# One load queue in order of need, and one chunk transposed by DMA, in a fused spectral filter and gated feed-forward kernel on Trainium2

## The chip, the cores and the metric

The kernel runs on one core of a Trainium2 chip. A core has five engines that run their own instruction streams and meet at semaphores: TensorE (PE, matmuls; PEld is its weight load), VectorE (DVE), ScalarE (ACT), GpSimd (POOL) and SyncE (SP, which here only issues DMAs). The metric is the device time in microseconds (us); the median of several runs is given. The profile describes one execution.

## The reference, cut to what matters

The input x has 2048 rows of 512 values, bfloat16. It is normalised by rows, and the result goes through two branches that are added to x: a filter in the two-dimensional Fourier domain, and a gated feed-forward layer with 1792 hidden values.

```python
xn = layernorm(x)                                  # rows of 512
A  = irfft2(rfft2(xn) * (w_r + 1j * w_i))          # 2048 x 257 spectrum
h  = gelu(xn @ w_gate) * (xn @ w_up)               # 2048 x 1792
B  = h @ w_down                                    # 2048 x 512
out = x + A + B
```

## The kernel before

The 2048 rows lie in SBUF as 16 tiles of 128 rows (x_sb, index j); four tiles make a chunk (index m, or b in the feed-forward part). Each tile is loaded in two halves of 64 partitions (load_x, with b = 0 and 1), because the halves come from different parts of the rows in HBM.

For each tile the row statistics are taken on DVE (ln_stat, L380; ln_aggr, L384 and L387), the reciprocal root on POOL (L388), and the normalised tile is written by DVE to xn (ln_norm, L392), a buffer of four tiles that lives in the tile cmx. Both branches want xn transposed, with the 512 values on partitions: the tile xnT. The first two tiles are transposed one by one (trans1, L1005, copied out of PSUM at L1012 and L1014), the others by trans (L402): PE transposes through an identity matrix into PSUM, then DVE (L412) or ACT (L414) copies to xnT. In this kernel xnT is laid out as [partition, 4 blocks of the 512 values, 2048 rows], so that the 512 rows of one chunk lie in a row for each of the four blocks.

From xnT the two branches go on. The feed-forward part takes, for each chunk b and each of 14 hidden blocks fc, a gate (four matmuls over the blocks of 512, L868, followed by gelu on ACT, L871) and an up (four matmuls, L883, multiplied with gelu's output on DVE, L889, into hT). The first six blocks of chunk 0 are done in two halves: first for the two first tiles, while tiles 2 and 3 are still being loaded and transposed. The products with w_down are made from sums and differences of blocks of hT and w_down (product, L772; sum_01, L705; sums_T, L734). The spectral part starts with butter (DVE, L422, L423, L425, L426), which adds and subtracts halves of xnT into the tile fold; unit_D (L439 to L443) is a matmul with a table fd, once a tile; units_A goes on with the table am (L471 to L474), and writes to the scratch scr1 in HBM, which load_tv reads back into tv. Later units B, C, E and F finish the branch, and unit_B's output is multiplied with the spectral weights W, loaded by load_W into a ring of four slots (32 loads on POOL's queue and 32 on SP's). keep_256 copies one column of a slot aside on POOL.

The order of the instructions on every engine is the order in which the program calls op. Semaphore waits are made from the keys that each op reads and writes. The main loop calls gate and up in turn, and after each of them a counter called the hook is raised; the list plan says which other calls are put in at which hook (at(h, call)). So a hook is a place in the order, about one gate or up apart. In chunk 0 the hooks 0 to 27 are passed, in chunk 1 those from 28. For the last chunk, m = 3, the norms are at hooks 28 and 29, the two transposes at 33 and 34, the butterflies at 35 and 36, and unit_D from 39.

The loads at the start are issued on two queues: SP takes one half of tiles 0 and 1, up weights for fc 0 to 2, one half of tiles 2 and 3, and up weights for fc 3 to 5; ACT takes the other halves and the gate weights in the same manner. SP then goes on with tiles 4 to 7, the table fd, weights 6 to 9, tiles 8 to 11, am, weights 10 to 13 and tiles 12 to 15. Before the first transposes PE does twelve matmuls on a tile of zeros (warm, L375).

Of the kernel before, what the change touches and what calls it, by code (L numbers as in the profile page):

```python
# [214 lines left out]
def bass_parallel_sum__spectral_gfnet__glu_gated_geglu__prompt_kernel(  # L215
# [27 lines left out]
    with ExitStack() as es:  # L243
# [4 lines left out]
        op = pr.op  # L248

        x_sb = sb("x_sb", [P, NJ, D], BF16)  # L250
        xnT = sb("xnT", [P, 4, S], F16)
        arena = sb("arena", [P, 8192], F16)
        am = arena[:, 0:3072].rearrange("p (j c) -> p j c", j=NJ)
        fold = [arena[:, 4096 + 2048 * i:6144 + 2048 * i].rearrange("p (a c) -> p a c", a=4) for i in range(2)]
# [94 lines left out]
        op("dve", lambda e: e.memset(dumm[:], 0.0), w=["dumm"])  # L349
        op("pool", lambda e: e.memset(mhalf[:], -0.5), w=["mhalf"])  # L350
        op("pool", lambda e: e.dma_start(ident[:], c_id.ap()), w=["ident"], dma=True)
        for b, eng, t, v, nm in ((0, "sp", wu_sb, wuv, "wu"), (1, "act", wg_sb, wgv, "wg")):
            load_x(0, 2, b, eng)
            load_w(t, v, nm, 0, 3, eng)
            load_x(2, 2, b, eng)
            load_w(t, v, nm, 3, 6, eng)
        op("act", lambda e: e.activation(warm_o[:], mhalf[:, 0:1], ACT.Gelu_apprx_tanh), r=["mhalf"], w=["warm_o"])
        load_x(4, 4, 0, "sp")
        load_x(4, 4, 1, "sp")
# [35 lines left out]
        def trans(m, dcs, jjs, eng="dve"):  # L395
            bk = take(1, 0.45, 1.2)
            def f(e):
                ins = None
                for a, dc in enumerate(dcs):
                    for c, jj in enumerate(jjs):  # L400
                        i = a * len(jjs) + c
                        ins = e.transpose(bank_h(bk)[:, i * P:(i + 1) * P], xn[:, jj, dc * P:(dc + 1) * P], ident[:])  # L402
                return ins
            op("pe", f, r=["ident"] + [("xn", jj) for jj in jjs], w=[("ps", bk)])
            w = len(jjs) * P
            c0 = m * 512 + jjs[0] * P
            n = len(dcs)
            dst = xnT[:, dcs[0]:dcs[0] + n, c0:c0 + w]
            src = bank_h(bk)[:, 0:n * w].rearrange("p (a c) -> p a c", a=n)
            ks = [("xnT", m, dc, jj) for dc in dcs for jj in jjs]  # L410
            if eng == "dve":
                op("dve", lambda e: e.tensor_copy(dst, src), r=[("ps", bk)], w=ks)  # L412
            else:
                op("act", lambda e: e.activation(dst, src, ACT.Copy), r=[("ps", bk)], w=ks)  # L414

        def butter(m, part):
            f = fold[m % 2]
            k = ("fold", m % 2)
            sl = slice(m * 512, (m + 1) * 512)
            xk = [("xnT", m, dc, jj) for dc in range(4) for jj in range(4)]  # L420
            if part == 0:
                op("dve", lambda e: e.tensor_tensor(ev1, xnT[:, 0:2, sl], xnT[:, 2:4, sl], ALU.add), r=xk, w=["ev1"])  # L422
                op("dve", lambda e: e.tensor_tensor(f[:, 2:4, :], xnT[:, 0:2, sl], xnT[:, 2:4, sl], ALU.subtract), r=xk, w=[k + (2,), k + (3,)])  # L423
            else:
                op("dve", lambda e: e.tensor_tensor(f[:, 0, :], ev1[:, 0, :], ev1[:, 1, :], ALU.add), r=["ev1"], w=[k + (0,)])  # L425
                op("dve", lambda e: e.tensor_tensor(f[:, 1, :], ev1[:, 0, :], ev1[:, 1, :], ALU.subtract), r=["ev1"], w=[k + (1,)])  # L426
# [225 lines left out]
               r=r + keys + [("x", j, 0), ("x", j, 1)], w=keys)  # L652

        eb7 = [early[:, 1792 * k:1792 * k + 1792].rearrange("p (f c) -> p f c", f=7) for k in range(4)]
        xb = xnT[:].rearrange("p d s -> p (d s)")
        cb = cmx[:]

        def ssum(b, k, f0, f1):
            if b == 2:
                return eb7[k][:, f0:f1, :]  # L660
            if k == 3:
                v = cb[:, 256 * f0:256 * f1]
            elif f1 <= 6:
                v = xb[:, 2048 * k + 256 * f0:2048 * k + 256 * f1]
            else:
                v = xb[:, 2048 * 3 + 256 * k:2048 * 3 + 256 * k + 256]
            return v.rearrange("p (f c) -> p f c", c=256)

        def s_keys(b, k, f0, f1):
# [45 lines left out]
        def s01(b, p, k, f0, f1):  # L715
            q = b == 0 and p == 1
            if k == 0 and b + p == 0:
                v = twh[:, 1024 + P * f0:1024 + P * f1]
            elif k == 0:
                v = arena[:, 7168 + P * f0:7168 + P * f1]  # L720
            else:
                assert f1 <= 4 or f0 >= 4
                o = P * (f0 % 4)
                if q and k in (1, 3):
                    v = fd[:, o:o + P * (f1 - f0)] if f0 >= 4 else dumm[:, o:o + P * (f1 - f0)]
                else:
                    row = 2 * (k == 2) + (f0 >= 4)
                    v = xb[:, 2048 * row + o:2048 * row + o + P * (f1 - f0)]
            return v.rearrange("p (f c) -> p f c", c=P)

        def sums_T(k):
# [127 lines left out]
        def gate(b, fc, jjs=(0, 1, 2, 3)):  # L859
            k = gun[0]  # L860
            n = len(jjs) * P
            c0 = b * 512 + jjs[0] * P
            bg = take(1, 0.0017 * n)

            def fn(e):
                ins = None
                for dc in range(4):
                    ins = e.matmul(bank(bg)[:, 0:n], wg_sb[:, dc, fc * P:(fc + 1) * P], xnT[:, dc, c0:c0 + n], start=(dc == 0), stop=(dc == 3))  # L868
                return ins
            op("pe", fn, r=[("wg", fc)] + [("xnT", b, dc, jj) for dc in range(4) for jj in jjs], w=[("ps", bg)])  # L870
            op("act", lambda e: e.activation(gl[k % 3][:, 0:n], bank(bg)[:, 0:n], ACT.Gelu_apprx_tanh), r=[("ps", bg)], w=[("gl", k % 3)])  # L871

        def up(b, fc, jjs=(0, 1, 2, 3), wait=False):
            k = gun[0]
            gun[0] += 1
            n = len(jjs) * P
            c0 = b * 512 + jjs[0] * P
            bu = take(1, 0.0017 * n, 2.2)

            def fn(e):  # L880
                ins = None
                for dc in range(4):
                    ins = e.matmul(bank(bu)[:, 0:n], wu_sb[:, dc, fc * P:(fc + 1) * P], xnT[:, dc, c0:c0 + n], start=(dc == 0), stop=(dc == 3))  # L883
# [55 lines left out]
            at(10 + 2 * i, (load_late, wd_sb[:, f0:f1, :], wdv[:, f0:f1, :], [("wd", fc) for fc in range(f0, f1)]))  # L939
        at(18, (load_late, be[:], c_be.ap(), ["be"]))  # L940
        at(19, (load_late, mm[:], c_mm.ap(), ["mm"]))
        for s, h0 in enumerate((20, 27, 34, 53, 61, 66, 70, 75)):
            for i, t in enumerate(load_W(s)):
                at(h0 + i // 2, t)
            at(89 + s // 2 if s > 3 else (47, 48, 49, 58)[s], (keep_256, s))
        cmv = c_cm.ap().rearrange("p (h r c) -> p h r c", h=NJ, r=2)
        for i, h0 in enumerate((54, 57, 63, 68)):
            hs = slice(4 * i, 4 * i + 4)
# [2 lines left out]
        for m in range(1, 4):  # L951
            a = (5, 15, 23)[m - 1]
            t = (16, 25, 33)[m - 1]
            for i in range(4):
                at(a + i, (ln_stat, 4 * m + i))
            at(a + 3, (ln_aggr, 4 * m, 4))
            for i in range(4):
                at(a + 5 + i // 2, (ln_norm, 4 * m + i))
            at(t, (trans, m, (0, 1), (0, 1, 2, 3)))
            at(t + 1, (trans, m, (2, 3), (0, 1, 2, 3), "act"))  # L960
            at(t + 2, (butter, m, 0))
            at(t + 3, (butter, m, 1))
        at(3, (butter, 0, 0))
# [35 lines left out]
        def trans1(j, engs):  # L999
            for i, eng in enumerate(engs):  # L1000
                bk = take(1, 0.12, 1.0)
                def f(e, i=i, bk=bk):
                    ins = None
                    for a in range(2):
                        ins = e.transpose(bank_h(bk)[:, a * P:(a + 1) * P], xn[:, j, (2 * i + a) * P:(2 * i + a + 1) * P], ident[:])  # L1005
                    return ins
                op("pe", f, r=["ident", ("xn", j)], w=[("ps", bk)])
                dst = xnT[:, 2 * i:2 * i + 2, j * P:(j + 1) * P]
                src = bank_h(bk)[:, 0:256].rearrange("p (a c) -> p a c", a=2)
                ks = [("xnT", 0, 2 * i + a, j) for a in range(2)]  # L1010
                if eng == "dve":
                    op("dve", lambda e, dst=dst, src=src: e.tensor_copy(dst, src), r=[("ps", bk)], w=ks)  # L1012
                else:
                    op("act", lambda e, dst=dst, src=src: e.activation(dst, src, ACT.Copy), r=[("ps", bk)], w=ks)  # L1014
# [108 lines left out]
```

## Time and profile before

| What | Value |
|---|---|
| median of 5 runs | 183.21 us (182.83 to 184.56) |
| profiled execution, own time | 183.1 us |
| its span (first to last instruction of the core) | 181.3 us |
| granted TensorE clock | 0.998 |
| PE, DVE, ACT, POOL busy | 175.1, 133.8, 95.6, 54.6 us |
| HBM read, written | 18.19 MB, 6.29 MB |
| DMA rate, mean over the span | 148 GB/s |

The profile page gives the busy time of each engine, the span in 40 slices, the DMA queues, the chain of work that ended last, the costliest groups of instructions and the DMA issues. The chain of work is followed back from the last instruction: each step leads to what released it, or to the instruction before it on its engine. Its shares say which engine the end waits for. Other views list the instructions in order of time with the idle time before them and its releaser, or sum busy times over chosen stretches. A busy PE is not PE at its peak, since matmuls are pipelined. A line number such as L337 can be that of a helper: all early loads are issued at L337.

### The profile page before, as it was taken

How to read it: one execution, taken by the hardware profiler on the slowest of the kernel's cores; microseconds unless marked ns; L12 is line 12 of the kernel's file. 1: busy time of each engine (PE TensorE's matmuls, PEld its weight loads, DVE VectorE, ACT ScalarE, POOL GpSimd, SP SyncE). 2: the span in 40 equal slices, each digit the busy share in tenths (PEclk: the TensorE clock that was granted, in tenths of full speed). 3: DMA queues.
4: the chain of work that ended last, by engine and by line, in shares of the span. 5: the costliest groups of instructions: out<-in, count | busy, mean ns of one | idle time of the engine just before them, and what ended most of it. 6: DMA issues, size and time to landing. Idle time of an engine off the chain costs nothing.

```text
span 181.3 us, 3873 instructions
## 1 busy us (share of the span) xinstructions
PE 175.1 (97%) x1438; PEld 110.1 (61%) x1438; DVE 133.8 (74%) x333; ACT 95.6 (53%) x160; POOL 54.6 (30%) x107
## 2 busy tenths in 40 slices
PE   7799999999999999999999999999999999999992
PEld 2378745564646556556655556556666767666882
DVE  1686989999386695786875749797877777897552
ACT  2244556767686631475656655336858677632110
POOL 2210081816130406276570000001354625640000
PEclk9999999999999999999999999999999999999999
DMA  4999999576846354477763121393155755742104
GB/s 130 279 256 303 323 277 325 144 213 178 227 107 158 101 149 125 116 185 210 206 175 91 58 61 58 113 278 133 25 98 104 126 116 91 117 74 42 33 2 116
DMA packets 26740, 26.84 MB, mean 148 GB/s; under 512 B 2929, under 2 KB 23537, under 8 KB 26593
## 3 DMA queue, kind: packets, MB, share of 16 engines
q1 hardware_dynamic: 20640, 17.91, 36.3%
q0 software_dynamic: 4272, 7.24, 17.5%
q10 hardware_dynamic: 1808, 1.44, 3.1%
q8 instruction: 11, 0.18, 0.4%
q14 instruction: 9, 0.07, 0.1%
HBM read 18.19 MB, written 6.29 MB: 135 GB/s over the span
## 4 chain that ended last, share of the span: by engine, by line
PE 80%; DVE 10%; DMA 5%; issue 2%; ACTq 1%; POOL 1%; ACT 0%; DVEq 0%
PE ps L772 23%; PE ps L883 22%; PE ps L868 22%; DMA wg<-in_B_w_gate_dram 5%; DVE st L380 3%; PE ps L596 2%; PE ps L826 2%; PE ps L624 2%; DVE hT L889 2%; PE ps L571 2%; PE ps L402 1%; DVE arena L734 1%; ACTq L337 1%; PE ps L471 1%; PE ps L442 1%
## 5 line engine op out<-in xcount | busy, mean ns | idle before, releaser
L868 PE MATMUL ps<-xnT,wg 128*128 128x512 f16 (+1 forms) x248 | 58.6, 359 | 0.9 <-ACT xnT L1014 0.5
L883 PE MATMUL ps<-xnT,wu 128*128 128x512 f16 (+1 forms) x248 | 58.6, 359 | 0.0
L889 DVE TENSOR_TENSOR hT<-ps,gl 128x512 bf16<-128x512 f32 (+1 forms) x62 | 39.4, 637 | 23.3 <-PE ps L883 17.5
L871 ACT ACTIVATE gl<-ps 128x512 bf16<-128x512 f32 (+1 forms) x62 | 34.5, 556 | 38.1 <-PE ps L868 37.0
L883 PEld LDWEIGHTS ps<-xnT,wu 128*128 128x128 bf16 x248 | 23.2, 98 | 19.3 <-issue 1.2
L868 PEld LDWEIGHTS ps<-xnT,wg 128*128 128x128 bf16 x248 | 23.2, 98 | 16.5 <-issue 1.4
L340 POOL DMA_DIRECT2D wring<-in_A_w_r_dram x32 | 18.6, 618 | 19.2 <-PE ps L772 9.8
L633 POOL COPY tv<-tv 1x128 bf16<-1x128 bf16 x16 | 5.4, 339 | 41.7 <-ACT tv L631 41.6
L772 PE MATMUL ps<-wd,hT 128*128 128x256 bf16 x112 | 14.4, 273 | 0.0
L852 POOL DMA_DIRECT2D x_sb<-tv x16 | 13.2, 865 | 3.4 <-DVE tv L845 2.4
L380 DVE BATCH_NORM_STATS2 st<-x_sb 128x6 f32<-128x512 bf16 x16 | 10.6, 683 | 3.8 <-DMA x_sb<-in_A_x_dram 3.8
L582 DVE TENSOR_TENSOR early<-early,wring 128x1024 bf16<-128x1024 f16 x16 | 10.3, 687 | 3.8 <-ACT early L577 3.8
L791 ACT ACTIVATE ps<-ps 128x256 f32<-128x256 f32 x16 | 5.9, 370 | 13.2 <-PE ps L772 13.1
L447 ACT ACTIVATE early<-ps 128x512 f16<-128x512 f32 x16 | 9.5, 596 | 5.7 <-PE ps L443 5.7
L772 PEld LDWEIGHTS ps<-wd,hT 128*128 128x128 bf16 x112 | 10.7, 98 | 2.5
L388 POOL TENSOR_TENSOR rstd<-vpe,mhalf 128x4 f32<-128x4 f32 (+2 forms) x6 | 5.0, 836 | 22.4 <-DVE vpe L387 22.4
L832 ACT ACTIVATE tv<-ps 128x512 bf16<-128x512 f32 x16 | 9.5, 595 | 3.6 <-PE ps L826 3.6
L772 PE MATMUL ps<-arena,xnT 128*128 128x256 f16 x91 | 11.4, 273 | 0.0
L631 ACT ACTIVATE tv<-ps 128x512 bf16<-128x512 f32 x16 | 9.5, 595 | 3.2 <-PE ps L624 3.2
L577 ACT ACTIVATE early<-ps 128x1024 f16<-128x1024 f32 x8 | 8.2, 1022 | 4.8 <-PE ps L571 4.8
L772 PEld LDWEIGHTS ps<-arena,xnT 128*128 128x128 f16 x91 | 8.6, 98 | 2.3 <-DVE tw L795 0.2
L651 DVE TENSOR_TENSOR x_sb<-ps,tw 128x256 bf16<-128x256 f32 x16 | 6.8, 422 | 2.9 <-PE ps L772 2.6
(118 smaller groups left out, 245.7 us busy)
## 6 DMA issues: line engine op xcount, KB each, us to landing
wring<-in_A_w_r_dram POOLq DMA_DIRECT2D x32, 64.2 KB, 3.1
wring<-in_A_w_i_dram SPq DMA_DIRECT2D x32, 64.2 KB, 3.0
tv<-scr SPq DMA_DIRECT2D x8, 256.0 KB, 3.8
scr<-early SPq DMA_DIRECT2D x8, 256.0 KB, 2.2
wring<-scr SPq DMA_DIRECT2D x4, 512.0 KB, 6.3
x_sb<-tv POOLq DMA_DIRECT2D x16, 128.0 KB, 2.8
scr<-early SPq DMA_DIRECT2D x15, 128.0 KB, 2.7
out_dram<-x_sb SPq DMA_DIRECT2D x28, 64.0 KB, 2.1
```

What stands on the lines that cost most here:

```text
L340: op(eng, lambda e: e.dma_start(dst, src), w=list(keys) + list(also), dma=True, after=[("pe", pr.cnt["pe"])])
L380: op("dve", lambda e: e.bn_stats(st[:, j, :], x_sb[:, j, :]), r=[("x", j, 0), ("x", j, 1)], w=[("st", j)])
L447: op("act", lambda e: e.activation(x4.rearrange("p (a c r) -> p a c r", a=2, r=4), bank(bk).rearrange("p (a r c) -> p a c r", a=2, r=4), A ...
L582: op("dve", lambda e, k=k: e.tensor_tensor(pp[i][k], xc[i], W[k][g % 4][:, :, :, 0:256], ALU.mult), r=[("xc", i)] + [key for c in range(2) ...
L631: op("act", lambda e: e.activation(z, bank(bk).rearrange("p (a c) -> p a c", a=4), ACT.Copy, scale=SC_E), r=[("ps", bk)], w=[zk] + (TVK if ...
L772: ins = e.matmul(o, st_(f), mv(f), start=(f == 0 and step in (0, 5)), stop=(f == 6), skip_group_check=True)
L832: op("act", lambda e: e.activation(o2, bank(bk), ACT.Copy), r=[("ps", bk)], w=[ok] + (TVK if j < 2 else []))
L852: op("pool", lambda e: e.dma_start(x_sb[:, j, :], ys, accum_op=ALU.add), r=[yk + (0,), yk + (1,), ("x", j, 0), ("x", j, 1)] + acc(j), w=ac ...
L868: ins = e.matmul(bank(bg)[:, 0:n], wg_sb[:, dc, fc * P:(fc + 1) * P], xnT[:, dc, c0:c0 + n], start=(dc == 0), stop=(dc == 3))
L871: op("act", lambda e: e.activation(gl[k % 3][:, 0:n], bank(bg)[:, 0:n], ACT.Gelu_apprx_tanh), r=[("ps", bg)], w=[("gl", k % 3)])
L883: ins = e.matmul(bank(bu)[:, 0:n], wu_sb[:, dc, fc * P:(fc + 1) * P], xnT[:, dc, c0:c0 + n], start=(dc == 0), stop=(dc == 3))
L889: op("dve", lambda e: e.tensor_tensor(hT[b % 2][:, fc, h0:h0 + n], bank(bu)[:, 0:n], gl[k % 3][:, 0:n], ALU.mult), r=[("ps", bu), ("gl", k ...
```

## The change

The change has three parts.

First, the loads at the start. Tiles 0 and 1 are loaded one by one, each with one half on SP's queue and the other on ACT's. All other early loads are issued on SP's queue, in this order: gate weights for fc 0 to 2, up weights for fc 0 to 2, tiles 2 and 3, gate weights and up weights for fc 3 to 5. What comes after them is as before.

Second, the layout of xnT is now [partition, 16 tiles, 4 blocks, 128 rows], so that a tile's four blocks, and a chunk's sixteen, lie together. All readers and writers of xnT are given the new indices, and so are the later uses of its memory for sums (ssum, s01).

Third, chunk 3 is no longer transposed by PE: one DMA with transpose, issued by SP at hook 29 behind the chunk's last norms, reads xn and writes the chunk's part of xnT. The W loads of slots 1 and 2 move from hooks 27 and 34 to 30 and 38, and keep_256 of slot 2 from hook 49 to 51.

```diff
-        xnT = sb("xnT", [P, 4, S], F16)
+        xnT = sb("xnT", [P, NJ, 4, P], F16)
...
-        for b, eng, t, v, nm in ((0, "sp", wu_sb, wuv, "wu"), (1, "act", wg_sb, wgv, "wg")):
-            load_x(0, 2, b, eng)
-            load_w(t, v, nm, 0, 3, eng)
-            load_x(2, 2, b, eng)
-            load_w(t, v, nm, 3, 6, eng)
+        for j in range(2):
+            load_x(j, 1, 0, "sp")
+            load_x(j, 1, 1, "act")
+        load_w(wg_sb, wgv, "wg", 0, 3, "sp")
+        load_w(wu_sb, wuv, "wu", 0, 3, "sp")
+        load_x(2, 2, 0, "sp")
+        load_x(2, 2, 1, "sp")
+        load_w(wg_sb, wgv, "wg", 3, 6, "sp")
+        load_w(wu_sb, wuv, "wu", 3, 6, "sp")
...
-            dst = xnT[:, dcs[0]:dcs[0] + n, c0:c0 + w]
-            src = bank_h(bk)[:, 0:n * w].rearrange("p (a c) -> p a c", a=n)
+            j0 = 4 * m + jjs[0]
+            dst = xnT[:, j0:j0 + len(jjs), dcs[0]:dcs[0] + n, :]
+            src = bank_h(bk)[:, 0:n * len(jjs) * P].rearrange("p (j a c) -> p j a c", a=n, c=P)
...
+        def trans_dma(m):
+            op("sp", lambda e: e.dma_start_transpose(xnT[:, 4 * m:4 * m + 4].rearrange("p j d c -> p (j d) c"), xn.rearrange("p a d -> p (a d)")),
+               r=[("xn", i) for i in range(4)], w=[("xnT", m, dc, jj) for dc in range(4) for jj in range(4)], dma=True)
...
-                op("dve", lambda e: e.tensor_tensor(ev1, xnT[:, 0:2, sl], xnT[:, 2:4, sl], ALU.add), r=xk, w=["ev1"])
-                op("dve", lambda e: e.tensor_tensor(f[:, 2:4, :], xnT[:, 0:2, sl], xnT[:, 2:4, sl], ALU.subtract), r=xk, w=[k + (2,), k + (3,)])
+                op("dve", lambda e: e.tensor_tensor(jac(ev1), xnT[:, js, 0:2, :], xnT[:, js, 2:4, :], ALU.add), r=xk, w=["ev1"])
+                op("dve", lambda e: e.tensor_tensor(jac(f[:, 2:4, :]), xnT[:, js, 0:2, :], xnT[:, js, 2:4, :], ALU.subtract), r=xk, w=[k + (2,), k + (3,)])
...
-                    ins = e.matmul(bank(bg)[:, 0:n], wg_sb[:, dc, fc * P:(fc + 1) * P], xnT[:, dc, c0:c0 + n], start=(dc == 0), stop=(dc == 3))
+                    ins = e.matmul(bank(bg)[:, 0:n], wg_sb[:, dc, fc * P:(fc + 1) * P], xnT[:, j0:j0 + len(jjs), dc, :], start=(dc == 0), stop=(dc == 3))
...
-        for s, h0 in enumerate((20, 27, 34, 53, 61, 66, 70, 75)):
+        for s, h0 in enumerate((20, 30, 38, 53, 61, 66, 70, 75)):
...
-            at(89 + s // 2 if s > 3 else (47, 48, 49, 58)[s], (keep_256, s))
+            at(89 + s // 2 if s > 3 else (47, 48, 51, 58)[s], (keep_256, s))
...
-            at(t, (trans, m, (0, 1), (0, 1, 2, 3)))
-            at(t + 1, (trans, m, (2, 3), (0, 1, 2, 3), "act"))
+            if m < 3:
+                at(t, (trans, m, (0, 1), (0, 1, 2, 3)))
+                at(t + 1, (trans, m, (2, 3), (0, 1, 2, 3), "act"))
+            else:
+                at(a + 6, (trans_dma, m))
```

More of the change, by code (lines that the diff above doesn't have):

```diff
@@ L400, in f @@
                     for c, jj in enumerate(jjs):
-                        i = a * len(jjs) + c
+                        i = c * len(dcs) + a
                         ins = e.transpose(bank_h(bk)[:, i * P:(i + 1) * P], xn[:, jj, dc * P:(dc + 1) * P], ident[:])
@@ L404, in trans @@
             op("pe", f, r=["ident"] + [("xn", jj) for jj in jjs], w=[("ps", bk)])
-            w = len(jjs) * P
-            c0 = m * 512 + jjs[0] * P
             n = len(dcs)
-            dst = xnT[:, dcs[0]:dcs[0] + n, c0:c0 + w]
-            src = bank_h(bk)[:, 0:n * w].rearrange("p (a c) -> p a c", a=n)
+            j0 = 4 * m + jjs[0]
+            dst = xnT[:, j0:j0 + len(jjs), dcs[0]:dcs[0] + n, :]
+            src = bank_h(bk)[:, 0:n * len(jjs) * P].rearrange("p (j a c) -> p j a c", a=n, c=P)
             ks = [("xnT", m, dc, jj) for dc in dcs for jj in jjs]
@@ L418, in butter @@
             k = ("fold", m % 2)
-            sl = slice(m * 512, (m + 1) * 512)
+            js = slice(4 * m, 4 * m + 4)
+            jac = lambda t: t.rearrange("p a (j c) -> p j a c", j=4)
             xk = [("xnT", m, dc, jj) for dc in range(4) for jj in range(4)]
             if part == 0:
-                op("dve", lambda e: e.tensor_tensor(ev1, xnT[:, 0:2, sl], xnT[:, 2:4, sl], ALU.add), r=xk, w=["ev1"])
-                op("dve", lambda e: e.tensor_tensor(f[:, 2:4, :], xnT[:, 0:2, sl], xnT[:, 2:4, sl], ALU.subtract), r=xk, w=[k + (2,), k + (3,)])
+                op("dve", lambda e: e.tensor_tensor(jac(ev1), xnT[:, js, 0:2, :], xnT[:, js, 2:4, :], ALU.add), r=xk, w=["ev1"])
+                op("dve", lambda e: e.tensor_tensor(jac(f[:, 2:4, :]), xnT[:, js, 0:2, :], xnT[:, js, 2:4, :], ALU.subtract), r=xk, w=[k + (2,), k + (3,)])
             else:
@@ L654, in bass_parallel_sum__spectral_gfnet__glu_gated_geglu__prompt_kernel @@
         eb7 = [early[:, 1792 * k:1792 * k + 1792].rearrange("p (f c) -> p f c", f=7) for k in range(4)]
-        xb = xnT[:].rearrange("p d s -> p (d s)")
+        xb = xnT[:].rearrange("p j d c -> p (j d c)")
         cb = cmx[:]
@@ L662, in ssum @@
                 v = cb[:, 256 * f0:256 * f1]
-            elif f1 <= 6:
+            else:
                 v = xb[:, 2048 * k + 256 * f0:2048 * k + 256 * f1]
-            else:
-                v = xb[:, 2048 * 3 + 256 * k:2048 * 3 + 256 * k + 256]
             return v.rearrange("p (f c) -> p f c", c=256)
@@ L727, in s01 @@
                     row = 2 * (k == 2) + (f0 >= 4)
-                    v = xb[:, 2048 * row + o:2048 * row + o + P * (f1 - f0)]
+                    v = xb[:, 512 * row + o:512 * row + o + P * (f1 - f0)]
             return v.rearrange("p (f c) -> p f c", c=P)
@@ L861, in gate @@
             n = len(jjs) * P
-            c0 = b * 512 + jjs[0] * P
+            j0 = 4 * b + jjs[0]
             bg = take(1, 0.0017 * n)
@@ L876, in up @@
             n = len(jjs) * P
-            c0 = b * 512 + jjs[0] * P
+            j0 = 4 * b + jjs[0]
             bu = take(1, 0.0017 * n, 2.2)
@@ L882, in fn @@
                 for dc in range(4):
-                    ins = e.matmul(bank(bu)[:, 0:n], wu_sb[:, dc, fc * P:(fc + 1) * P], xnT[:, dc, c0:c0 + n], start=(dc == 0), stop=(dc == 3))
+                    ins = e.matmul(bank(bu)[:, 0:n], wu_sb[:, dc, fc * P:(fc + 1) * P], xnT[:, j0:j0 + len(jjs), dc, :], start=(dc == 0), stop=(dc == 3))
                 return ins
@@ L958, in bass_parallel_sum__spectral_gfnet__glu_gated_geglu__prompt_kernel @@
                 at(a + 5 + i // 2, (ln_norm, 4 * m + i))
-            at(t, (trans, m, (0, 1), (0, 1, 2, 3)))
-            at(t + 1, (trans, m, (2, 3), (0, 1, 2, 3), "act"))
+            if m < 3:
+                at(t, (trans, m, (0, 1), (0, 1, 2, 3)))
+                at(t + 1, (trans, m, (2, 3), (0, 1, 2, 3), "act"))
+            else:
+                at(a + 6, (trans_dma, m))
             at(t + 2, (butter, m, 0))
@@ L1007, in trans1 @@
                 op("pe", f, r=["ident", ("xn", j)], w=[("ps", bk)])
-                dst = xnT[:, 2 * i:2 * i + 2, j * P:(j + 1) * P]
+                dst = xnT[:, j, 2 * i:2 * i + 2, :]
                 src = bank_h(bk)[:, 0:256].rearrange("p (a c) -> p a c", a=2)
```

## The prediction

> **What bounds the kernel now.** I read the page first: the busy table, then the chain of work that ended last.
>
> ```profile
> span 181.3 us, 3873 instructions
> PE 175.1 (97%) x1438; PEld 110.1 (61%) x1438; DVE 133.8 (74%) x333; ACT 95.6 (53%) x160; POOL 54.6 (30%) x107
> ...
> PE 80%; DVE 10%; DMA 5%; issue 2%; ACTq 1%; POOL 1%; ACT 0%; DVEq 0%
> ```
>
> TensorE (PE) carries 80% of the chain, so PE instructions taken away in its stretches count in full. The 5% of DMA is one piece. The same chain in order of time shows it, and the pieces that the change deletes:
>
> ```profile
> 2.53 9.08 DMA wg<-in_B_w_gate_dram
> 11.65 0.61 PE ps L868 x4
> ...
> 47.11 0.45 PE ps L402 x8
> ...
> 48.75 0.45 PE ps L402 x8
> ```
>
> The reader is to see that the chunk's PE transposes at 47.11 and 48.75 (L402) lie on the chain. The start, from the timeline:
>
> ```profile
> 1.19 5.30 PE L375 MATMUL ps<-dumm 128*128 128x512 f16 x12 [1.19 <-DVE dumm L349]
> ...
> 4.22 0.69 DVE L380 BATCH_NORM_STATS2 st<-x_sb 128x6 f32<-128x512 bf16 x1 [3.08 <-DMA x_sb<-in_A_x_dram]
> ...
> 6.79 0.38 PE L1005 MATMUL ps<-ident,cmx 128*128 128x128 f16 x4 [0.30 <-DVE cmx L392]
> ...
> 8.48 0.60 PE L868 MATMUL ps<-xnT,wg 128*128 128x256 f16 x4 [0.52 <-ACT xnT L1014]
> ...
> 11.65 0.61 PE L868 MATMUL ps<-xnT,wg 128*128 128x256 f16 x4 [0.40 <-DMA wg<-in_B_w_gate_dram]
> ```
>
> The column order is start, duration, engine, line, and in brackets the idle time before with its releaser. Useful work starts when the first x lands (4.22); the first gate starts at 8.48; the fourth gate waits for the second block of gate weights. Last, the stage in which the last chunk is transposed:
>
> ```profile
> 44.04 0.72 DVE L392 TENSOR_SCALAR cmx<-x_sb,ag,rstd 128x512 f16<-128x512 bf16 x2
> ...
> 51.03 0.68 DVE L422 TENSOR_TENSOR cmx<-xnT 128x1024 f16<-128x1024 f16 x1
> ...
> 54.77 0.22 PE L439 MATMUL ps<-fd,arena 128*128 128x128 f16 x1
> ```
>
> Norms end at 44.76, the first butterfly of the chunk (L422) starts at 51.03, and the first matmul that needs the butterflies (unit_D, L439) at 54.77. These three times set how long a DMA may take.
>
> **What the Trainium skill says.** (1) "DMA: Bandwidth & Descriptors", section Queues, rings and completion order: each of the 16 engines goes round-robin between queues that have work, packet by packet. The trace agrees: the two halves of x tiles 0 and 1 (128 KB each, issued at 0.74) take 2.9 us on ACT's queue and 3.5 us on SP's, with weights queued behind in both. (2) The same page, section Issuing engines are not separate DMA queues: a second issuing engine saves only issue time. Here the ACT queue ends at 11.6, and with SP's load queue alone the core moved 353 GB/s in 14 to 16 us and 372 in 20 to 22, against 259 in 12 to 14. (3) "VectorE: DVE Perf Modes", section The three transpose paths: a 128x128 block costs 390 ns on TensorE and 1309 ns as a DMA. The trace has eight PE transposes in 0.45 us of chain, 56 ns each, since they are pipelined; it has no DMA transpose. (4) A price from the DMA page, section Latency and other measured facts: a DMA transpose was measured at 261 GB/s. No run here shows it yet.
>
> **Part 1, the order of the loads.** Tile 0 comes alone, 64 KB on each queue, then tile 1, then weights and tiles 2 and 3 on SP only. Three loads move from ACT's queue to SP's, so SP issues ten loads up to tiles 4 to 7, of some 0.6 us each: all by about 7 us, ahead of the bytes, which arrive at 262 GB/s (the window from 2 to 14 us). ACT's table load and its warm-up activation come some 1.2 us earlier, which nobody waits for.
> - First x: data flows from about 2.1 (DMA share is 0 before 2 us). 128 KB at 262 GB/s is 0.5, plus 0.4 to signal: tile 0 at about 3.1, tile 1 at about 3.8.
> - That lets norm 0 end near 5.6 instead of 6.65, but PE's twelve warm-up matmuls run to 6.49 and ident lands at 1.25 + 5.0 = 6.25 (issue table, 5.0 us), so the first transposes move only from 6.79 to about 6.42. The second ones move from 7.56 to 6.86: norm 1 (ending near 6.4) no longer holds them, only PE's own order does. ACT must then copy three banks in a row: 6.73 + 0.66 + 0.38 = 7.77, and the first gate starts at 7.87 against 8.48. Gain 0.61. It stands while tile 0 comes before about 3.5.
> - The fourth gate: six pieces of 0.437 after 7.87 is 10.49. In the one queue 1.70 MB lie up to the second gate block: 2.1 + 6.5 + 0.3 = 8.9, in time. The up block (2.08 MB) arrives at 10.3, its matmul wants it at 10.93. So the wait at 11.65 goes, and the gain there is 11.65 - 10.49 = 1.16.
> - What is late next: norm 3 on DVE. It moves only with the first gain (POOL's rstd, 0.7, lies in that chain): 12.93 - 0.61 = 12.32, whereas PE would want its transposes at 13.41 - 1.16 = 12.25. They start at 12.38, and 1.03 is left.
> - Further on: from 16.8 to 33.1 the chain is mostly DVE, in order behind PE work, so it shifts too. Loads have room: tiles 4 to 7 estimated at 12.3, wanted at 18.3; the fc 6 to 9 up weights landed at 18.3 in the kernel before and are wanted at 20.2. I take 1.0. Bounds: 0 (tile 0 lands at 4.2, norm 3 keeps the rest) and 1.3.
>
> **Part 2, the DMA transpose of chunk 3.** Removed: 16 PE transposes, 2 x 0.45 = 0.90 on the chain; a DVE copy (0.68) and an ACT copy (1.02), both beside PE, worth nothing by themselves. Added: one 512 KB DMA on SP, waiting for the four norms. On SP the chunk-1 stores (2.61 from 41.82, done 44.43) are issued ahead of it, so its wait holds nobody; behind it stand load_tv of chunk 1 (two 256 KB loads, wanted only by unit_B after 74) and the W loads moved from hooks 27 and 34 to 30 and 38, wanted by the products after 79 and by POOL's keep_256 from 59.6. POOL's half of the W loads moves likewise; keep_256 of slot 2 goes two hooks later. All at nothing, covered by 10 us and more; if that cover were gone, POOL alone would wait.
> - How long may it take? Without the transposes DVE is ready for the butterfly at 51.03 - 0.90 = 50.13, which is 5.4 after 44.76. Butterflies end at 52.99 and unit_D starts at 54.77, so another 1.7 is slack for PE: the free budget is 7.1 us. Behind the waiting butterfly in DVE's queue are the products with gelu (L889) and the first sums; DVE has idle times of 1.51 and 1.39 at 58.45 and 62.35, which take up such a delay.
> - How long will it take? From below: 512 KB at 261 GB/s is 2.0, plus the 2.1 that a 64 KB store takes here, 4.1. The chunk-1 stores ahead of it are landing until about 47 (2.7 each); with them I take 5. From above: sixteen blocks of 1309 ns in a row, 21 us (an estimate from that page). I take the low end since one small DMA is mostly latency, which is paid once; plain loads of 512 KB take 6.3 and 7.2 here among others of their kind.
> So the gain is 0.90, and the DMA hides.
>
> **Part 3, the layout of xnT.** Gates and ups read four runs of 128 instead of 512 in a row; butterflies read and write runs of 128 or 256. L705 reads runs of 128 and does 896 elements in 0.62, L734 runs of 256, 1792 in 1.09: 0.69 and 0.61 ns an element, beside 0.66 for the butterfly now. So DVE costs nothing more. For PE the trace has no such moving operand; I take 0, with 10 ns a matmul at most: 496 x 0.01 = 5 us. Bound below: 0. If the butterflies fell to half speed, four in the DVE stretch would cost about 4 x 0.6 = 2.4. All other reshaped indices name as many bytes as before.
>
> **Sum.** 1.0 + 0.90 = 1.9. The profiled execution took 183.10 (181.3 of it span); the median is 183.21. 183.1 - 1.9 = 181.2, and 181.3 against the median.
>
> **Rivals.**
> - The transpose lands between 7.1 and 9.0 after the norms: PE stalls at unit_D and pays back up to 1.9. At 8.0 that is 0.9, hence 182.2. For: the 6 to 7 us of plain 512 KB loads. Against: these share engines with others.
> - The early gain is lost in part (tile 0 late, or a later load or DVE holds PE): 0.3 + 0.9 gives 182.0; with nothing, 182.3. For: warm-up and ident already cap it. Against: no PE wait after 11.65 names a load.
> - The other side: the crossbar transpose is slow, nearer to its price per block. The place is DVE's butterfly of chunk 3, with unit_D behind it. PE pays each us over 7.1; from 9.0 the change is a loss, from 9.9 a measurable one. At 12 us: 181.3 + 4.9 = 186.2; at 21: 195. For: the skill's price per block, and no DMA transpose in the trace. Against: the 261 GB/s.
> - The layout costs PE or DVE (Part 3): 2.4 would give 183.7.
> That the change doesn't do what it says is no case: the dependencies in the code are full.
>
> **Chances.** A measurement tells 0.5% (0.9 us) from no change. Forecast (180.3 to 182.0) 0.60; late but paying 0.10; early gain lost 0.12; slow transpose 0.14; layout 0.04 (a quarter of it slower). Faster (below 182.3): 0.60 + 0.05 + 0.08 = 0.73. Slower (above 184.1): 0.13 + 0.01 = 0.14. Same: 0.13. The range runs from 180.3 (1.3 early gives 181.0, and 0.68 more should the DVE copy count in DVE's full stretch from 52 to 57) to 183.6, which holds all but the slow transpose and the worst of the layout.
>
> **What would show it.** Right: first statistics near 3.2, first gate near 7.9, no DMA wait at the fourth gate, chunk-3 transposes gone, the butterfly of chunk 3 near 48.8 to 49.2 with little or no wait, gate matmuls still 359 ns in the mean. Wrong: a long DVE idle before L423's pair in chunk 3 put down to the xnT DMA, with PE idle before unit_D; a first gate still at 8.4; longer gate or butterfly rows.

## The result and the profile after

The changed kernel took a median of 182.79 us (43 runs) against 183.13 us for the kernel before (80 runs). The ratio is 0.9971, with a 95% interval of 0.9959 to 0.9984: 0.3% faster, where 1% had been forecast. The median lies above the 180.3 to 182.0 us that got the largest chance, though below the range's upper end of 183.6. Twelve of the 80 runs before, at 184.2 to 184.6 us, seem to be of a kind whose granted clock is near 0.99 instead of 1.00, and they count in the ratio, while four such runs of the changed kernel don't; without them on either side the means differ by 0.32 us, 0.2%, and the ratios of the experiments can be up to 0.3% too low in the same way. The profiled execution took 183.37 us (span 181.6), 0.6 above the median; it gives the places, while the sizes of the totals are taken from the ratios.

The page of the changed kernel answers to the lines shown first: span, busy times, and the chain that ended last.

```profile
span 181.6 us, 3845 instructions
PE 174.5 (96%) x1422; PEld 109.5 (60%) x1422; DVE 133.0 (73%) x332; ACT 94.7 (52%) x159; POOL 54.8 (30%) x107
...
PE 74%; DVE 11%; DMA 8%; SPq 2%; issue 2%; POOL 1%; ACT 1%; DVEq 0%
```

PE has 16 instructions fewer, as planned, but its share of the chain fell by 6 points and DMA's rose from 5% to 8%. The chain in order of time (start, length, what) names the two transfers.

```profile
5.28 7.01 DMA wu<-in_B_w_up_dram
...
44.94 7.41 DMA xnT<-cmx
```

So the old wait for gate weights was replaced by one for up weights, and the transpose became a piece of the chain itself. The timeline of the start:

```profile
3.27 0.69 DVE L384 BATCH_NORM_STATS2 st<-x_sb 128x6 f32<-128x512 bf16 x1 [2.14 <-DMA x_sb<-in_A_x_dram]
...
6.29 0.63 PE L1014 MATMUL ps<-ident,cmx 128*128 128x128 f16 x4
...
7.98 0.60 PE L874 MATMUL ps<-xnT,wg 128*128 128x256 f16 x4 [0.52 <-ACT xnT L1023]
...
9.29 0.69 DVE L384 BATCH_NORM_STATS2 st<-x_sb 128x6 f32<-128x512 bf16 x1 [1.61 <-DMA x_sb<-in_A_x_dram]
...
10.60 0.60 PE L874 MATMUL ps<-xnT,wg 128*128 128x256 f16 x4
...
12.33 0.61 PE L889 MATMUL ps<-xnT,wu 128*128 128x256 f16 x4 [1.13 <-DMA wu<-in_B_w_up_dram]
```

The first gate is 0.50 earlier and the fourth gate 1.05 earlier, at 10.60. But the fourth up, directly behind it, waits until 12.33. In the kernel before it ran sooner:

```profile
12.10 0.60 PE L883 MATMUL ps<-xnT,wu 128*128 128x256 f16 x4
```

All that was won is gone at that point, and 0.2 more. The stage of the transpose:

```profile
44.94 2.87 SPq L420 DMA_TRANSPOSE xnT<-cmx  x1
...
52.37 0.69 DVE L430 TENSOR_TENSOR cmx<-xnT 128x1024 f16<-128x1024 f16 x1 [1.91 <-DMA xnT<-cmx]
...
54.39 0.23 PE L447 MATMUL ps<-fd,arena 128*128 128x128 f16 x1
```

The transpose takes 7.4 us to land, DVE stands for 1.91 before the butterfly, and unit_D starts at 54.39 instead of 54.77. Since the kernel came into the stage 0.23 late, it has gained 0.6 of the 0.9. A third loss stands in a place of which the prediction says nothing:

```profile
97.25 0.41 PE L579 MATMUL ps<-tv,be 64*64 64x256 f16 x8
98.10 0.63 PE L604 MATMUL ps<-early,cmx 64*64 64x256 bf16 x16 [0.43 <-ACT gl L877]
```

Here unit_C (L604) waits for gelu's read of a PSUM bank (ACT, L877). In the kernel before the same pair has no such wait:

```profile
97.59 0.41 PE L571 MATMUL ps<-tv,be 64*64 64x256 f16 x8
97.83 0.61 PE L596 MATMUL ps<-early,cmx 64*64 64x256 bf16 x16
```

To sum this up, and to compare the experiments by stage, the table takes the DVE products hT<-ps,gl (62 of them, in the same order in all kernels) as marks, and gives how much later each starts than in the profiled execution before. It is worked out from the traces.

| Kernel | mark 7 (15.92) | mark 21 (43.44) | mark 28 (62.35) | mark 36 (90.48) | mark 39 (99.45) | mark 62 (166.66) |
|---|---|---|---|---|---|---|
| changed kernel | +0.24 | +0.14 | -0.36 | -0.33 | +0.30 | +0.29 |
| early_only | +0.17 | +0.16 | +0.16 | +0.16 | +0.16 | +0.16 |
| dma_only | -0.22 | -0.32 | -1.12 | -1.12 | -0.49 | -0.49 |
| after_banks | +0.18 | +0.07 | -0.56 | -0.56 | -0.56 | -0.56 |
| trans_clear | +0.75 | +0.66 | -0.14 | -0.15 | +0.48 | +0.48 |
| old_loads | +1.58 | +1.48 | +0.68 | +0.68 | +0.68 | +0.68 |
| two_queues | -0.47 | -0.57 | -1.37 | -1.37 | -1.37 | -1.37 |
| split_block | -0.08 | -0.18 | -0.98 | -0.98 | -0.98 | -0.98 |
| hold_rest | -0.37 | -0.26 | -1.06 | -1.06 | -1.06 | -1.06 |
| both_fixes | +0.38 | +0.28 | -0.52 | -0.07 | -0.07 | -0.07 |
| split_hold | -0.55 | -0.65 | -1.45 | -1.45 | -1.45 | -1.45 |
| both_chunks | -0.56 | -1.32 | -2.35 | -0.72 | -0.72 | -0.72 |
| all_together | +0.17 | -0.59 | -1.62 | -1.62 | -1.62 | -1.62 |

Read along a row: a difference between two columns is what the stage between them gained or lost. Between marks 7 and 28 lies the transpose of chunk 3, between 36 and 39 the bank wait. The first column varies by more than half a microsecond between executions with the same load order, mostly with the landing of the loads; the later steps repeat to 0.1. Each row is one execution.

### The profile page after: what moved, and what is told of

Read it like the earlier page. It is cut to its first block, busy times and chain, and to the rows that moved or that the text cites. A ratio compares the mean times of both kernels' runs of the same rounds, so it can differ in the third digit from the quotient of the medians.

```text
span 181.6 us, 3845 instructions
## 1 busy us (share of the span) xinstructions
PE 174.5 (96%) x1422; PEld 109.5 (60%) x1422; DVE 133.0 (73%) x332; ACT 94.7 (52%) x159; POOL 54.8 (30%) x107
## 4 chain that ended last, share of the span: by engine, by line
PE 74%; DVE 11%; DMA 8%; SPq 2%; issue 2%; POOL 1%; ACT 1%; DVEq 0%
PE ps L778 23%; PE ps L889 20%; PE ps L874 19%; DMA xnT<-cmx 4%; DMA wu<-in_B_w_up_dram 4%; DVE st L384 3%; SPq L337 2%; PE ps L604 2%; PE ps L832 2%; PE ps L632 2%; DVE hT L895 2%; PE ps L579 1%; DVE arena L740 1%; DVE cmx L430 1%; PE ps L406 1%
## 5 line engine op out<-in xcount | busy, mean ns | idle before, releaser
L877 ACT ACTIVATE gl<-ps 128x512 bf16<-128x512 f32 (+1 forms) x62 | 34.5, 556 | 39.9 <-PE ps L874 39.9
L590 DVE TENSOR_TENSOR early<-early,wring 128x1024 bf16<-128x1024 f16 x16 | 10.3, 688 | 3.8 <-ACT early L585 3.8
L778 PEld LDWEIGHTS ps<-wd,hT 128*128 128x128 bf16 x112 | 10.7, 98 | 2.5
L778 PE MATMUL ps<-arena,xnT 128*128 128x256 f16 x91 | 11.4, 273 | 0.0
```

The costliest lines, as they stand in the source:

```text
L590: op("dve", lambda e, k=k: e.tensor_tensor(pp[i][k], xc[i], W[k][g % 4][:, :, :, 0:256], ALU.mult), r=[("xc", i)] + [key for c in range(2) ...
L778: ins = e.matmul(o, st_(f), mv(f), start=(f == 0 and step in (0, 5)), stop=(f == 6), skip_group_check=True)
```

## The experiments

**One part at a time.** early_only puts chunk 3 back on PE:

```diff
-            if m < 3:
-                at(t, (trans, m, (0, 1), (0, 1, 2, 3)))
-                at(t + 1, (trans, m, (2, 3), (0, 1, 2, 3), "act"))
-            else:
-                at(a + 6, (trans_dma, m))
+            at(t, (trans, m, (0, 1), (0, 1, 2, 3)))
+            at(t + 1, (trans, m, (2, 3), (0, 1, 2, 3), "act"))
```

> Parts 1 and 3 alone: the new load order and the new layout of xnT, with chunk 3 transposed by PE and the W loads and keep_256 at their old hooks. Theory (the early gain is given back): the first gate starts near 8.0, the fourth gate no longer waits, but the fourth up waits for its block of up weights until about 12.3, so PE is 0.2 to 0.3 us later than in the kernel before at 15 us and stays so: 183.3 to 183.4 beside 183.1. Rival (the early part gains and the loss comes from the DMA transpose): 182.6 or less.

Measured: ratio 0.9991 (0.9963 to 1.0020), the up block landing 6.9 after its issue at 5.3, and a constant +0.16 from mark 7 to the end; the median is 183.34 us, as expected. The early part gives its gain back. The constant row also shows that the layout of xnT costs nothing, and the gate and up groups have 359 ns in the mean in both kernels.

dma_only puts the old loads back (the four load lines of the kernel before).

> Parts 2 and 3 alone: the DMA transpose of chunk 3 and the new layout, with the old order of the early loads. Theory (the transpose is late by 1.9 us but pays 0.6, of which a PSUM bank wait near 98 us takes 0.6 back): about 0.2 to 0.3 us less than after, 182.5. Rival (the transpose itself costs time in the end): 183.1 or more.

Measured: ratio 0.9992 (0.9961 to 1.0022), too wide to tell it from the changed kernel. By stage it is clear: the transpose landed after 6.5 us instead of 7.4, so the stage gained the whole 0.90, from -0.22 to -1.12, and not only 0.6; then 0.63 were lost at the same unit_C.

**The bank wait.** after_banks only changes the program's bookkeeping: two requests for a PSUM bank (the helper take) where the transposes had been.

```diff
                 at(a + 6, (trans_dma, m))
+                at(t, (take, 1, 0.45, 1.2))
+                at(t + 1, (take, 1, 0.45, 1.2))
```

> The changed kernel, with the program's bookkeeping of PSUM banks told of two transposes at hooks 33 and 34 that are not issued, so that all later work gets the banks that it had in the kernel before. Theory (the 0.6 us lost at unit_C near 98 us come from a bank that gelu still reads, because two bank requests fewer shift the rotation): the wait of L604 for ACT's gelu is gone and the time falls by 0.5 to 0.6 against after, to about 182.2. Rival (the loss at 98 us is a chance of that execution or comes from the W loads): no change, 182.8.

Measured: ratio 0.9952 (0.9929 to 0.9974), median of the runs that count 182.55. The timeline of after_banks has the pair with no wait:

```profile
97.03 0.41 PE L579 MATMUL ps<-tv,be 64*64 64x256 f16 x8
97.27 0.61 PE L604 MATMUL ps<-early,cmx 64*64 64x256 bf16 x16
```

In the table the step from mark 36 to 39 is 0.00, against +0.63 in all three kernels that drop the transposes and keep the planner as it is (the changed kernel, dma_only, trans_clear). The cause is shown for these executions: take gives out the bank that its own model of time says comes free first, and without the two requests it gave unit_C a bank that gelu was still reading. The total fell by 0.2% (0.9971 to 0.9952, and the intervals overlap) and not by the 0.3% that was expected; why the rest is missing isn't shown.

**The transpose's neighbours.** trans_clear moves what was issued beside and behind the transpose: the W loads of slot 1, half of which go on POOL's queue, and load_tv of chunk 1, which follows on SP's.

```diff
-        for s, h0 in enumerate((20, 30, 38, 53, 61, 66, 70, 75)):
+        for s, h0 in enumerate((20, 36, 38, 53, 61, 66, 70, 75)):
...
-            at(h + 8 + (4 if m < 1 else 0), (load_tv, m))
+            at(h + 8 + (4 if m < 1 else 0) + (7 if m == 1 else 0), (load_tv, m))
```

> The changed kernel with the DMA transpose's neighbours moved away: load_tv of chunk 1 from hook 30 to 37 and the W loads of slot 1 from hook 30 to 36. Theory A (the 7.4 us from issue to landing hold some 2 us of waiting for the loads that share the engines behind the last data packet): 5.3 to 5.8 us to landing, DVE's wait before L430 falls from 1.9 to below 0.4, unit_D of chunk 3 starts 0.3 earlier, time 0.2 to 0.4 below after. Theory B (the crossbar's own price, or the stores of chunk 1 ahead of it): 7 us or more again and the same time.

The timeline, and the landing time from the view of the tile xnT:

```profile
45.45 1.79 SPq L420 DMA_TRANSPOSE xnT<-cmx  x1
...
50.89 0.68 DVE L430 TENSOR_TENSOR cmx<-xnT 128x1024 f16<-128x1024 f16 x1
```

```profile
DMA to landing us min/median/max: 3.8/3.8/3.8
```

3.8 us instead of 7.4, no wait before the butterfly, and the stage gains 0.89. So the neighbours made the transpose slow, by more than expected. The chunk-1 stores were still ahead of it in this run, so they aren't what did it. The time itself did not fall (ratio 0.9988, 0.9963 to 1.0013): this expectation missed. In the profiled execution the early stage was late, +0.75; whether it was so in the other runs isn't on record.

The experiment moves two kinds of neighbours at once, but two later traces show more. In both_chunks, described below, load_tv of chunk 0 stands right behind chunk 3's transpose on SP's queue, while the next W loads on POOL's queue are issued only from 45.95 on, 2.5 us after the transpose. The first two lines are of the changed kernel, the others of both_chunks:

```profile
44.39 2.39 POOL L340 DMA_DIRECT2D wring<-in_A_w_r_dram  x4 [2.81 <-PE ps L874]
...
44.94 2.87 SPq L420 DMA_TRANSPOSE xnT<-cmx  x1
```

```profile
43.47 1.33 SPq L422 DMA_TRANSPOSE xnT<-cmx  x1
44.98 1.18 SPq L337 DMA_DIRECT2D tv<-scr  x2
```

Here load_tv follows after 1.5 us, sooner than in the changed kernel (3.0), and the transpose lands after 3.75 us; in all_together, with the same order, after 3.71. Loads behind the transpose on its own queue are therefore not enough to slow it. What the three slow executions have and the fast ones lack are the four W loads of 64 KB on POOL's queue: in the changed kernel their packets ran from 45.89 to 50.49, all through the transpose's own. No experiment moved these alone, so they are what is left as the cause, by themselves or together with load_tv.

**Sum of the parts.** old_loads has the transpose, both repairs and the load order of the kernel before; both_fixes is the same with the new load order.

> The DMA transpose of chunk 3 with its neighbours moved away (load_tv of chunk 1 to hook 37, W loads of slot 1 to hook 36), the bank bookkeeping as in the kernel before, the new layout, and the old order of the early loads. Theory: the three findings add up. The transpose lands after about 4 us and hides, its 0.90 of PE time is saved in full, no bank wait takes 0.63 back, and the early stage is as in the kernel before: 182.2 to 182.3, ratio 0.995. Rival (the stages are not additive, something later takes the gain): 182.7 or more.

> The changed kernel with its new load order, plus the two repairs of the later stages: the transpose's neighbours moved away and the bank bookkeeping as before. Theory: the loss of the early stage stays (up block landing at 12.2 to 12.8, the kernel 0.2 to 0.7 late at 15 us), the transpose pays its full 0.89 and the banks cost nothing: 182.4 to 182.6, against 183.2 for trans_clear and 182.6 for after_banks. Rival (the early loss hides in the later gains): 182.2 or less, equal to split_block.

Measured: ratios 0.9951 (0.9923 to 0.9979) and 0.9971 (0.9946 to 0.9997), that is 182.2 and 182.6 on a base of 183.1. Both agree with their theories by the ratio, though the intervals overlap and the median of both_fixes' counted runs is 182.8, 0.2 above its forecast. The profiled execution of old_loads stands 1.58 behind at mark 7; its matmuls ran at half pace from about 9 to 12.4 us (see the last section), and its later stages repeat the others'. both_fixes loses 0.45 between marks 28 and 36, at unit_B, whose tv loads are issued at 68.8 instead of 66.8.

**Why the up block is late.** Four kernels change the loads on top of both repairs. hold_rest lets SP go on with tiles 4 to 7 only when the early weights have landed.

```diff
-        load_x(4, 4, 0, "sp")
+        op("sp", lambda e: e.dma_start(x_sb[0:64, 4:8, :], xv[0, :, 4:8, :]), w=[("x", j, 0) for j in range(4, 8)], dma=True, after=[pr.writer[("wu", 5)]])
```

> As the changed kernel with the transpose's neighbours moved away and the bank bookkeeping as before, but SP issues tiles 4 to 7 and all loads after them only once the up weights for fc 3 to 5 have landed, so nothing follows them on the DMA engines. Only their landing is of interest; later loads will be late and the time longer. Theory A (engines that are done early go on with later loads and take bandwidth from the slowest engine): the up block lands near 10.3 instead of 12.3. Theory B (the slowest engine needs that long for its own share): 11.8 or later again.

The view of the tile wu, of that DMA alone:

```profile
L337 SPq DMA_DIRECT2D wu<-in_B_w_up_dram x1: 507/507/507, 5.3 to 5.3; - x1
...
DMA to landing us min/median/max: 5.7/5.7/5.7
```

It lands at 11.0. In five profiled executions with loads behind it (the changed kernel, early_only, after_banks, trans_clear and both_fixes) it landed 6.9 to 7.5 after issue, at 12.2 to 12.8. So 1.2 or more come from the later loads, and about 0.7 over the predicted 10.3 remain with nothing behind: the answer lies between the two theories. It rests on one execution, of 182.02 us; the longer time that was expected did not come. The trace holds sixteen completion signals for each load. In the changed kernel those of the up block come at 10.36 (the first), 10.7 (half of them), 11.66 (the fifteenth) and 12.28 (the last); in hold_rest all sixteen come from 10.27 to 11.01. So it is a late last part that the wait is for, not the block's mean rate. That engines which are done early go on with later loads is a reading that fits this; the trace doesn't say which engine a signal is of.

two_queues keeps SP and ACT for the weights and only separates tiles 0 and 1. split_block cuts the late blocks:

```diff
-        load_w(wg_sb, wgv, "wg", 3, 6, "sp")
-        load_w(wu_sb, wuv, "wu", 3, 6, "sp")
+        load_w(wg_sb, wgv, "wg", 3, 4, "sp")
+        load_w(wu_sb, wuv, "wu", 3, 4, "sp")
+        load_w(wg_sb, wgv, "wg", 4, 6, "sp")
+        load_w(wu_sb, wuv, "wu", 4, 6, "sp")
```

> As old_loads, but tiles 0 and 1 are loaded one by one (four loads of 64 KB instead of two of 128 KB), with the weights still on the two queues SP and ACT. Theory (the early stage is bound by the time that 2 MB and the slowest DMA engine take, in whatever order): the first gate starts near 8.0, but the fourth gate or up still waits for its block, which lands near 12; no gain against old_loads beyond 0.2. Rival (one queue alone made the loads late): both blocks land by 11 and the time is 0.5 or more below old_loads, 181.7.

> As old_loads, but with the new order of the early loads on SP, and in it the weights for fc 3 to 5 cut into fc 3 (gate, then up) and fc 4 to 5 (gate, then up). Theory: the up block of fc 3 now lies 0.26 MB further ahead and lands near 11, so its wait of 1.1 to 1.6 falls to below 0.4 and the early stage is 0.5 better than in the changed kernel: 181.9 to 182.2. Rival (the smaller pieces with 256-byte rows move more slowly and the wait only moves to the next block): no better than old_loads, 182.3 or more.

Measured: two_queues 0.9958 (0.9933 to 0.9983), no better than old_loads, though its profiled execution was 0.47 ahead of the kernel before at mark 7, its blocks landing at 10.5 and 11.4; whether the second queue helps stays open. split_block: 0.9927 (0.9899 to 0.9955), median 181.78 in seven runs, 0.1 below the forecast. Its up block of fc 3 landed at 10.3, and the wait for it is gone. But the wait has moved to the next block, as the rival said, the up weights of fc 4 and 5, which land at 12.83:

```profile
12.88 0.61 PE L891 MATMUL ps<-xnT,wu 128*128 128x256 f16 x4 [0.85 <-DMA wu<-in_B_w_up_dram]
```

It is 0.85 instead of 1.1 to 1.6, since that block is wanted later; at mark 7 the kernel stands 0.32 before the changed kernel, not 0.5.

**Versions built on this.** split_hold is split_block with the later loads held until the gate weights of fc 3 land (the hold_rest line with `("wg", 3)`). both_chunks is split_block with chunk 2 transposed by DMA too (`m < 2`, W loads of slot 0 to hook 33, load_tv of chunk 0 to 34).

> As split_block, but SP issues tiles 4 to 7 and all later loads only when the gate weights of fc 3 have landed, near 9.7 us. Theory (later loads take bandwidth from the last early block: 12.2 us with them behind it, 11.0 when held back): the up block of fc 3 lands near 9.6 to 10.0 and its wait of 0.8 goes, 0.3 to 0.7 below split_block, if the later loads, some 4 us later, still come in time. Rival (weights for fc 6 to 9, wanted at 20 us, are then late): no better than split_block, 181.8 or more, with PE waiting for wu or wg near 20 us.

> As split_block, with chunk 2 transposed by DMA as well, at hook 21 behind its norms (W loads of slot 0 from hook 20 to 33 and load_tv of chunk 0 to hook 34, so that nothing follows the transpose on SP's queue). Theory (a transpose without neighbours lands in 3.8 us): another 0.90 of PE transposes and a DVE copy go, the butterfly of chunk 2 finds its data in time: 180.9 to 181.1. Rival (DVE, full from 26 to 44 us, sets the end there and not PE, or the chunk-0 stores hold the transpose): 0.4 or less below split_block.

split_hold: 0.9931 (0.9906 to 0.9955). Its up block of fc 3 lands at 9.7 and that of fc 4 and 5 at 11.6, PE's wait is gone, and the profiled execution is 0.47 ahead of split_block at mark 7; the totals don't tell the two apart. Whether the holding did it isn't shown: the fc 3 block lands at 9.9 in both_chunks, where nothing is held, and at 10.4 in all_together, where it is. both_chunks: 0.9920 (0.9892 to 0.9948). Both transposes landed in 3.8 to 4.3 us (only the one of chunk 2 has nothing behind it on SP's queue), and the table shows the second 0.8 (marks 7 to 21) and then a loss of 1.63 behind mark 28. The waits of its PE name it (engine, line, releaser: total, times, longest):

```profile
PE ps L581 <- DMA tv<-scr: 1.6, 1, 1.6
```

unit_B now came to the tile tv before its last load, which took 6.2 us to land. Earlier kernels had slack there, but for both_fixes. The runs that count fall in two groups of eight, 180.7 to 181.4 and 182.3 to 183.1 us. The profiled one, 182.36, is of the upper group; the lower group is where the forecast stood, so the wait may be missing there, but no trace of it was kept.

all_together takes split_hold and both_chunks and moves the W loads of slot 2 behind the last load_tv (hook 48, keep_256 of that slot at 57).

> The findings put together: split weights for fc 3 to 5, later loads held until the gate weights of fc 3 have landed, chunks 2 and 3 transposed by DMA with nothing behind them on SP's queue (W loads of slot 0 at hook 33, slot 1 at 36, load_tv of chunks 0 and 1 at 34 and 37), and the W loads of slot 2 moved behind the last load_tv (hook 48, its keep_256 at 57), since in both_chunks unit_B waited 1.6 us for the tile tv that load_tv fills. Theory: no wait of unit_B for tv, early stage as in split_hold (1.45 ahead at the end), 0.90 more for chunk 2: 180.8 to 181.1. Rival (the late W loads now hold unit_B's products or POOL, or tv comes late all the same): 181.8 or more, with a wait of 1 us near 73.

Measured: ratio 0.9878 (0.9834 to 0.9923), median 181.39 in six runs, and no wait of unit_B in the trace. The base of that comparison is 183.3; against the 183.1 of the others 181.39 is 0.991. The mean lies 0.64 below split_hold's, clear of the scatter, and 0.45 below both_chunks', which is not clear of it. The median is 0.3 above the forecast: in the profiled execution the early stage was 0.7 behind split_hold's at mark 7, with a 0.6 wait for the up weights of fc 4 and 5, the same scatter again.

## Why the prediction was wrong

- First gate: forecast 7.87, measured 7.98. The reasoning by PE's warm-up and ACT's copies held; ident, which was taken to land at 6.25, came at 3.85 and no longer mattered.
- Fourth gate: forecast 10.49, measured 10.60. It held.
- **The step that failed first: "The up block (2.08 MB) arrives at 10.3, its matmul wants it at 10.93."** It arrived at 12.3. (By the shapes it is 2.10 MB, which adds 0.1.) The mean rate that it used was right: 264 GB/s from 2 to 11.6 us before, 260 from 2 to 12.3 after. But the sum took the queue for strictly one block after the other, while a block counts as landed when the last of its sixteen signals has come. The first of them came at 10.36, the last at 12.28; with the later loads held back, at 11.0. In place of +1.0 the early part cost 0.2. Tiles 2 and 3 were late too: by the same sum (1.31 MB) they would land near 7.4, and they landed at 8.4 and 9.2. Had the kernel before's own landings been used, 11.6 and 12.0 for about the same bytes, the step would have come out right.
- **The term that was mis-sized: "with them I take 5"** for the transpose. It took 7.4 in the changed kernel and 3.8 without neighbours (the lower bound was 4.1). The step behind it is "All at nothing" for the loads that were moved: they had slack for themselves, but what they would do to the transpose wasn't asked. By both_chunks it is the W loads on POOL's queue beside it that are left as the cause, and "POOL's half of the W loads moves likewise" brought them there.
- "The free budget is 7.1 us" held closely: 6.5 us cost nothing (dma_only), 7.4 cost 0.3.
- "So the gain is 0.90": shown, 0.89 to 0.90 with the transpose in time. Of the rivals, "lands between 7.1 and 9.0" and "The early gain is lost in part" happened, both in one kernel; the chances give no case for the two together.
- The layout at 0: shown by early_only.
- The 259 GB/s in 12 to 14 us is no stretch with two queues, since ACT's load queue had ended at 11.6. The conclusion, that one queue loses no rate, still agrees with the 264 and 260 GB/s above.
- The bank wait of 0.63 was missing altogether. Removing an instruction that asks a planner for a buffer can change everything handed out after it.

For the profiled executions the account closes: +0.24 early, -0.60 for the transpose (0.90 less 0.3), +0.63 for the bank, together +0.27, and the spans are 181.3 and 181.6. It doesn't close for the totals: in the runs the changed kernel is 0.3 faster, not 0.3 slower. Its profiled execution is slower than most of its runs, and what these do otherwise isn't on record.

The Trainium skill's 261 GB/s ("DMA: Bandwidth & Descriptors", Latency and other measured facts) agrees: in trans_clear the transpose's 2048 packets of 256 bytes take from 46.76 to 48.81, 256 GB/s, and the estimate of 4.1 built on it stands beside 3.7 to 4.3 measured without the W loads beside it. Its 1309 ns a block ("VectorE: DVE Perf Modes", The three transpose paths) isn't additive: sixteen blocks in one DMA took 3.8 us, not 21.

## What to carry to other kernels

Ordering loads by need can only move the wait to the next block: compare with landings that the trace already shows, and count what is queued behind a block too. A transfer that is put on the path should be kept clear of its neighbours; those on another queue, issued at the same time, are the ones left under suspicion here, while loads behind it and stores ahead of it on its own queue did no harm by themselves. When an instruction is taken out of a kernel with planned buffers, keep its buffer request or look for new waits far behind the change.

## What was not expected of the hardware

The 3.6 us by which the transpose lands later in the changed kernel than in trans_clear can be split by its packets. The first of 256 bytes starts 1.97 after the issue instead of 1.31; the packets take 3.19 instead of 2.05; and from the end of the last one to the landing it is 2.24 instead of 0.48. The packets of the W loads on POOL's queue (4112 bytes, 0.35 us each in the mean) run in that time. Why the end report is late isn't shown. The 16 KB packets of load_tv start 0.26 before the transpose's last packet ends, but in all_together they start 0.10 before, and there the report comes after 0.47.

SP's queue is held 1.3 to 2.9 us by issuing one such transpose, against mostly 0.5 to 0.7 for a plain load.

In old_loads' profiled execution PE stood 1.09 us before its first transposes and then ran its gates and ups 0.85 apart until 12.4 us, instead of 0.44; the granted clock of that trace is 0.56 from 9 to 10 us, 0.50 from 10 to 12 and 0.73 from 12 to 13, and 0.991 over the whole span. In dma_only's it stood 1.36 and ran at full pace, with a clock of 1.00 throughout. What decides this stays open.
